# Second half of the reloaded T4: issued from the GpSimd queue instead of the SP queue

## Chip, cores and metric

One Trainium2 chip, one core. The metric is the device time of one execution in microseconds; the median of the runs shown is what counts.

## What is computed

A transformer block on x of 2048 tokens by 1024 features: layernorm, linear attention with 32 heads, residual; then layernorm and a token-mixing MLP (2048 tokens to 3584 hidden units and back), residual. The last part, cut from the reference:

```python
def _B_ref(x, w1, b1, w2, b2):
    h = _layernorm(x, axis=-1)
    u = _gelu(jnp.einsum("bsd,sf->bdf", h, w1) + b1)
    y = jnp.einsum("bdf,fs->bds", u, w2) + b2
    return transpose(y)                      # back to tokens by features
h2 = h + _B_ref(_layernorm(h), B_w1, B_b1, B_w2, B_b2)
```

The change concerns the second product, u with w2, which fills the time from about 390 us to the end.

## The kernel before

The second product is done by a Strassen-like scheme with seven products of half-size blocks (`Product7`, methods p1 to p7). Its moving operands are the two halves of the hidden activation, gE (even rows of 128) and gO (odd rows), and three differences of them, T2, T3 and T4. T2 stays in SBUF (gT2). T3 (product 7) and T4 (product 4) don't both fit: each is computed once, half by half, in `derived`, written to DRAM (tiles called parked), and read back when its product is due. There are two SBUF tiles for them, gs0 and gs1, one per half of the contraction (7 of 14 chunks of 128, 896 KB each); in the profile both are "gs". `reload(m, h)` reads half h of T3 (m = 7) or T4 (m = 4) back into its tile. A reload must wait until PE has read the tile's earlier content.

The outputs come in row blocks of 256 tokens, called p; two of them form a `Quad`. The first quad is done by itself, the other three by `Quad.run2` with u = 1, 2, 3. In run2 two of the seven products of a quad (1 and 5) and two more (2 and 3) are done once more by the same scheme over both row blocks: the inner steps, in order in1, in5, in2, in3. Between the inner matmuls `interleave` fills in the matmuls of products 6, 7 and 4: product 7 (from T3) beside in2, the first half of product 4 (T4, gs0) beside in3, and the second half (T4, gs1) beside in1 of the next quad. For the last quad that second half comes at the very end.

The weights of w2 come in "even" and "odd" rows of 128 interleaved: `even` has two buffers (896 KB each, the tile is called wq), which are reloaded for the next quad by `next2`, as soon as product 7 of this quad has read them, with `load_w2(p, 0, hd)`. In run2 the calls stand in this order, at the end of in2:

```python
            nxt = nxt()          # next2(u + 1): two even weight rows on SP; nothing in the last quad
            load("in2")          # the second half of T4 into gs1
```

Engines are written with prefixes: `hd` is SyncE (SP) with its instructions kept in program order, `nc.gpsimd` is the GpSimd engine (POOL). `Held.__getattr__` (line 230) is the line under which all kept instructions appear. DMAs issued on SP run on the queue that the profile calls q1 hardware_dynamic, those on POOL on q0 software_dynamic.

The outputs are added to the residual, which is already in the output tensor, by accumulating DMAs on POOL (line 484, in `Mixer2.out`): 30 of them, 128 rows of 1 KB each. They go through four output buffers (`ots`, pieces of a wq tile), filled by ScalarE (line 487) or VectorE (line 491). The order of the POOL queue beyond kept instructions is set by the scheduler of the language.

Of the kernel before, what the change touches and what calls it, by code (L numbers as in the profile page):

```python
# [30 lines left out]
def kernel(  # L31
# [12 lines left out]
    nc = tc.nc  # L44
# [116 lines left out]
    def load_w2(p, second, q=nc.sync):  # L161
        q.dma_start(
            (odd[p] if second else even[p % 2]),
            B_w2[:, p * 2 * P:(p + 1) * 2 * P].rearrange("(k two p) s -> p k two s", two=2, p=P)[:, :, second, :],
        )
# [64 lines left out]
            return (lambda *a, **kw: pin(op(*a, **kw))) if self.always or getattr(Held, self.key) else op  # L230

    dve, pe, act = Held(nc.vector), Held(nc.tensor), Held(nc.scalar, key="scalar")
    hv, ht, hs, hd = (Held(e, True) for e in (nc.vector, nc.tensor, nc.scalar, nc.sync))

    class Inner:
        banks = 4
# [1352 lines left out]
    parked = {}  # L1589

    def gs_tile(m, h):
        t = g2pool.tile([P, H2, CW], FP16, tag=f"gs{h}", name=f"gs{h}")
        gs[m, h] = t
        now = [gs.get((m, i)) for i in range(2)]
        gmov[m] = lambda k: now[k // H2][:, k % H2, :]
        return t
# [9 lines left out]

        return [partial(make, h) for h in range(2)]

    def reload(m, h):
        hd.dma_start(gs_tile(m, h)[:], parked[m, h][:])  # L1610

    make_t3 = derived(7, lambda sl: (gT2[:, sl, :], gE[:, sl, 0:CW]))
    make_t4 = derived(4, lambda sl: (gO[:, sl, 0:CW], gT2[:, sl, :]))
# [23 lines left out]
    def loads(u):  # L1637
        def load(at):
            last = 2 * u + 2 >= NSP
            if at == "in1":  # L1640
                if u == 1:
                    reload(7, 0)
                reload(7, 1)
                for p in (2 * u + 2, 2 * u + 3):
                    if 4 <= p < NSP:
                        load_w2(p, 1, hd)
            elif at == "p7":
                reload(4, 0)
            elif at == "in2":
                reload(4, 1)  # L1650
            elif at == "in3":
                if not last:
                    reload(7, 0)
        return load
# [70 lines left out]
```

## Time and profile before

| what | value |
|---|---|
| median of 3 runs | 562.45 us (562.22 to 563.06) |
| the profiled execution's own time | 562.69 us |
| its span, first to last instruction | 560.9 us |
| PE busy | 552.3 us |
| POOL busy | 28.0 us, 30 of its instructions the accumulating stores of 0.93 us mean |
| reloads (gs<-parked) | 12 on SP, 896 KB each, median 5.1 us from issue to landing |
| even weight rows (wq<-in_B_w_dram, 896 KB) | 12 on SP, median 7.2 us |
| accumulating stores (out_dram<-wq, 128 KB) | 30 on POOL, median 6.0 us |

The profile is of one execution, so sums are made against its own time. Instants are microseconds from the start of the span. An engine's row in a timeline is: start, length, engine, line, operation, output<-input, shape, how many, and in square brackets how long the engine idled before it and what released it. For a DMA the length on SP or POOL is that of issuing it, not of moving the data; "to landing" is from its issue to its completion.

### The profile page before, as it was taken

Reading aid. Unit: us, or ns where it says so; the run is one execution under the profiler, and the core shown is the slowest. Engines: PE = TensorE matmul, PEld = TensorE weight load, DVE = VectorE, ACT = ScalarE, POOL = GpSimd, SP = SyncE. Lnnn points to the kernel's source line nnn. Section 1 sums busy time; section 2 is a strip of 40 time slices with the busy share of each in tenths; the row PEclk is TensorE's granted clock in tenths of the full one; section 3 lists DMA queues with packets and bytes.
Section 4 is the critical chain, followed back from the end, with each engine's and each line's share of the span. In section 5 each row is a group of like instructions: output and inputs, shape, how many; then the busy total and the mean of one; then the engine's idle time right before and its main releaser. Section 6 shows DMA issues by size and latency. Waiting matters only on the chain.

```text
span 560.9 us, 8812 instructions
## 1 busy us (share of the span) xinstructions
PE 552.3 (98%) x3323; PEld 316.0 (56%) x3339; DVE 427.6 (76%) x836; ACT 290.8 (52%) x617; POOL 28.0 (5%) x38
## 2 busy tenths in 40 slices
PE   8999999999999999999999999999999999999997
PEld 3444444454444444456666766666445666666665
DVE  6898888544776688889989789888997878648643
ACT  5747677766766877645546465564211412413322
POOL 1000000000000000000000000000002103103112
PEclk9999999999999999999999999999999999999999
DMA  9933332115765851103140340422959749849336
GB/s 306 295 75 76 84 86 39 19 48 194 218 205 134 256 186 76 75 1 106 47 150 24 128 151 1 151 61 72 230 198 284 213 142 295 207 130 282 87 94 132
DMA packets 84203, 77.92 MB, mean 139 GB/s; under 512 B 15666, under 2 KB 76096, under 8 KB 84160
## 3 DMA queue, kind: packets, MB, share of 16 engines
q1 hardware_dynamic: 79104, 72.76, 42.8%
q0 software_dynamic: 4384, 3.95, 4.8%
q10 hardware_dynamic: 672, 0.66, 0.3%
q8 instruction: 26, 0.43, 0.3%
q14 instruction: 17, 0.14, 0.1%
HBM read 61.62 MB, written 12.58 MB: 132 GB/s over the span
## 4 chain that ended last, share of the span: by engine, by line
PE 92%; DMA 4%; DVE 2%; ACT 1%; issue 1%; SPq 0%; DVEq 0%; ACTq 0%
PE psI L230 23%; PE acc_t L230 18%; PE psC L230 14%; PE psB L230 8%; PE psC L940 4%; PE psB L940 4%; PE psA L940 4%; DMA gs<-parked 4%; PE psA L342 2%; PE psB L342 2%; PE acc_t L1226 2%; PE psE L940 2%; PE psC L342 2%; PE acc_t L864 2%; PE psA L230 1%; PE kvps L893 1%
## 5 line engine op out<-in xcount | busy, mean ns | idle before, releaser
L230 PEld LDWEIGHTS <-is 128*128 128x128 f16 x736 | 71.8, 98 | 31.2 <-DVE hi L230 0.4
L230 PEld LDWEIGHTS <-sa 128*128 128x128 f16 x606 | 59.2, 98 | 27.1
L230 PEld LDWEIGHTS <-wq 128*128 128x128 bf16 (+1 forms) x496 | 48.5, 98 | 29.2 <-issue 2.1
L230 PE MATMUL acc_t<-wo_sb,pqT 128*128 128x512 f16 x256 | 55.6, 379 | 0.0
L484 POOL DMA_DIRECT2D out_dram<-wq x30 | 26.1, 931 | 527.4 <-ACT wq L487 497.1
L230 PE MATMUL acc_t<-xnT,wq_sb 128*128 128x512 bf16 x188 | 43.1, 379 | 0.2
L230 PEld LDWEIGHTS <-pqT 128*128 128x128 bf16 x256 | 25.0, 98 | 30.5 <-issue 0.6
L193 DVE TENSOR_SCALAR e_sb<-e_sb 128x512 bf16<-128x512 bf16 x64 | 18.5, 290 | 28.8 <-ACT e_sb L189 28.2
L230 DVE TENSOR_TENSOR t<-psI,t 128x256 f32<-128x256 f32 (+1 forms) x45 | 20.8, 475 | 22.2 <-PE psI L230 21.0
L189 ACT ACTIVATE e_sb<-acc_t 128x512 bf16<-128x512 f32 x40 | 23.9, 597 | 24.5 <-PE acc_t L230 12.0
L230 PE MATMUL psC<-gs,wq 128*128 128x512 f16 x140 | 34.1, 379 | 1.0 <-DMA gs<-parked 1.0
L940 PEld LDWEIGHTS <-xs 128*128 128x128 f16 x208 | 20.0, 98 | 23.3 <-DVE xs L926 1.3
L230 PEld LDWEIGHTS <-wq_sb 128*128 128x128 bf16 x192 | 18.5, 98 | 23.0 <-issue 1.3
L230 PE MATMUL psC<-hT,sa 128*128 128x512 f16 x112 | 31.2, 379 | 0.0
L230 PE MATMUL psI<-hi,is 128*128 128x256 f16 x200 | 30.0, 273 | 0.0
L230 PE MATMUL psB<-hT,sa 128*128 128x512 f16 x112 | 29.7, 379 | 0.0
L230 DVE BATCH_NORM_STATS2 hst<-acc_t 128x6 f32<-128x512 f32 x32 | 21.4, 692 | 9.1 <-ACT h_bf L230 8.9
L940 PE MATMUL psA<-wkv,xnT 128*128 128x512 bf16 x99 | 26.4, 379 | 0.3
L940 PEld LDWEIGHTS <-xnT 128*128 128x128 bf16 x156 | 15.3, 98 | 18.5 <-issue 0.2
L230 DVE TENSOR_TENSOR e<-psI,es 128x256 f32<-128x256 f32 x20 | 8.5, 424 | 21.8 <-PE psI L230 21.8
L230 PE MATMUL psC<-hT,wq 128*128 128x512 f16 x96 | 24.6, 379 | 0.0
L230 ACT CAST h_bf<-acc_t 128x512 bf16<-128x512 f32 x32 | 18.4, 581 | 11.9 <-PE acc_t L230 11.7
(227 smaller groups left out, 1089.9 us busy)
## 6 DMA issues: line engine op xcount, KB each, us to landing
wq<-in_B_w_dram SPq DMA_DIRECT2D x14, 1024.0 KB, 7.8
wq<-in_B_w_dram SPq DMA_DIRECT2D x12, 896.0 KB, 7.2
gs<-parked SPq DMA_DIRECT2D x12, 896.0 KB, 5.1
xr<-in_A_x_dram SPq DMA_DIRECT2D x16, 256.0 KB, 5.2
rdb<-rd_dram SPq DMA_DIRECT2D x32, 128.0 KB, 3.9
out_dram<-h_bf SPq DMA_DIRECT2D x16, 256.0 KB, 2.0
x_sb<-in_A_x_dram SPq DMA_DIRECT2D x15, 256.0 KB, 3.0
out_dram<-wq POOLq DMA_DIRECT2D x30, 128.0 KB, 6.0
```

What stands on the lines that cost most here:

```text
L189: pin(nc.scalar.activation(e_sb[:], src, ACT.Exp))
L193: pin(nc.vector.tensor_scalar(e_sb[:], e_sb[:], 1.0, PHI_EPS, ALU.min, ALU.add))
L230: return (lambda *a, **kw: pin(op(*a, **kw))) if self.always or getattr(Held, self.key) else op
L342: pe.matmul(ps[:, cols], lhsT=lhs[:, k, :], rhs=mv(k)[:, cols], start=(start and k == 0), stop=(k == self.nk - 1), skip_group_check=True,)
L484: nc.gpsimd.dma_start(to, ot[:, a:b], accum_op=ALU.add)
L864: mm = nc.tensor.matmul(pp[:, 0:CW], lhsT=xnT[:, kt, i * P:(i + 1) * P], rhs=wkv[:, kt, c * CW:(c + 1) * CW], start=(kt == 0), stop=(kt == ...
L893: pin(nc.tensor.matmul(kv_ps[b][:, sl, :], lhsT=pks[i % NPK][:, j * P:(j + 1) * P], rhs=vaugs[i % NVA][:, j, :], start=False, stop=(i == N ...
L940: pin(nc.tensor.matmul(ps[:], lhsT=lhs[:, k, :], rhs=rhs[:, k, :], start=(start and k == 0), stop=(k == hk2 - 1), skip_group_check=True,))
L1226: nc.tensor.matmul(qp[:, 0:SW], lhsT=wq_sb[:, kt, j * P:(j + 1) * P], rhs=xnT[:, kt, u * SW:(u + 1) * SW], start=(kt == 0), stop=(kt == ND ...
```

## The change

The second half of T4 is issued with `nc.gpsimd` in place of `nc.sync`. As before, the instruction is kept in program order among the kept ones of its engine; it is the only kind of kept DMA on GpSimd. The tile, its source, its size and what it must wait for stay as they are. It is called three times, for u = 1, 2 and 3. In the last quad no even rows are loaded.

```diff
-    hv, ht, hs, hd = (Held(e, True) for e in (nc.vector, nc.tensor, nc.scalar, nc.sync))
+    hv, ht, hs, hd, hg = (Held(e, True) for e in (nc.vector, nc.tensor, nc.scalar, nc.sync, nc.gpsimd))
...
-    def reload(m, h):
-        hd.dma_start(gs_tile(m, h)[:], parked[m, h][:])
+    def reload(m, h, q=hd):
+        q.dma_start(gs_tile(m, h)[:], parked[m, h][:])
...
             elif at == "p7":
                 reload(4, 0)
             elif at == "in2":
-                reload(4, 1)
+                reload(4, 1, hg)
```

## The prediction

> **What bounds the kernel now.** I read the page's first and fourth parts, then the chain of waits in order of time, then the PE, SP and POOL timelines around its gaps, then the DMA answers in stretches of half a microsecond to two.
>
> ```profile
> span 560.9 us, 8812 instructions
> PE 552.3 (98%) x3323; PEld 316.0 (56%) x3339; DVE 427.6 (76%) x836; ACT 290.8 (52%) x617; POOL 28.0 (5%) x38
> PE 92%; DMA 4%; DVE 2%; ACT 1%; issue 1%; SPq 0%; DVEq 0%; ACTq 0%
> ```
>
> TensorE is busy 98% of the span; only a PE wait removed or added moves the end. The chain names one tile's transfer, and the list of waits gives its true price: "PE psC L230 <- DMA gs<-parked" is 1.9 us, 2 times. The PE timeline has the two places:
>
> ```profile
> 472.53 0.93 PE L230 MATMUL psI<-gE,wq 128*128 128x256 f16 x7
> 474.40 1.02 PE L230 MATMUL psC<-gs,w2o 128*128 128x512 f16 x4 [0.94 <-DMA gs<-parked]
> 515.05 1.02 PE L230 MATMUL psC<-gs,wq 128*128 128x512 f16 x4 [0.97 <-DMA gs<-parked]
> ```
>
> The reader is to see that PE was ready at 473.46 (474.40 less 0.94) and 514.08, and waited for T4's second half, the tile gs1. The 10.34 us that the chain gives this transfer is its whole flight, nearly all beside PE work. The SP timeline shows why it is late:
>
> ```profile
> 458.27 0.34 SPq L230 DMA_DIRECT2D gs<-parked  x1
> 461.31 2.64 SPq L230 DMA_DIRECT2D wq<-in_B_w_dram  x2
> 464.01 8.28 SPq L230 DMA_DIRECT2D gs<-parked  x2
> ```
>
> gs1 is issued at 464.01, right behind two even rows, which land at 466.6 and 471.5 (5.3 and 8.0 us after issue). gs1 lands 10.3 us after issue, though the same 896 KB takes 4.6 to 5.4 us where no row is ahead. The third use has no rows: issued at 544.87 (second line below is POOL's), landed 5.2 us later, needed at 553.99 by the chain. So there is 1.9 us to win in all, 0.34% of the time.
>
> POOL's timeline shows the queue that the transfer moves to:
>
> ```profile
> 463.56 1.75 POOL L484 DMA_DIRECT2D out_dram<-wq  x2 [20.91 <-ACT wq L487]
> 466.47 1.76 POOL L484 DMA_DIRECT2D out_dram<-wq  x2 [1.16 <-ACT wq L487]
> 504.18 1.75 POOL L484 DMA_DIRECT2D out_dram<-wq  x2 [20.68 <-ACT wq L487]
> 507.09 1.75 POOL L484 DMA_DIRECT2D out_dram<-wq  x2 [1.16 <-DMA wq<-in_B_w_dram]
> 544.84 1.75 POOL L484 DMA_DIRECT2D out_dram<-wq  x2 [20.68 <-ACT wq L487]
> 547.75 1.75 POOL L484 DMA_DIRECT2D out_dram<-wq  x2 [1.15 <-ACT psC L403]
> ```
>
> Around each use POOL issues four accumulating stores, in two pairs, at 0.86 us each. The window 549.5 to 552 shows their own pace, with nothing on SP's queue:
>
> ```profile
> q0 software_dynamic: 468, 0.42, 112.5%
> q1 hardware_dynamic: 1, 0.00, 0.0%
> ```
>
> 468 packets in 2.5 us, so about 190 a microsecond; one store is 144 packets (128 rows and 16 more, from 576 for four).
>
> [...] from 471.5 to 473.5 both queues moved 92 packets, rows of 7 KB on q1 against 1 KB on q0. [...] the DMA share of 0.91 to 1.15 from 464 to 478 agrees that there is no idle engine to win. [...] q0's first packets come 4.6 us after the issue at 463.56 (DVE busy from 462.08 to 468.20), but those of the lone store at 554.08, with DVE idle, after about 1.4 us.
>
> **The change part by part.** Three reloads leave SP and join POOL. The two builds have the same instruction order on PE, DVE and ACT. On POOL each reload stands directly behind the four stores above.
>
> *Issue, SP side.* Removed: three issues of about 0.33 us. SP's next work is the reload of T3's first half at about 472.0, which waits for PE. Cover: that wait. Gain 0. The rows gain nothing either, because gs1 stood behind them.
>
> *Issue, POOL side.* POOL is free for it at 466.47 + 1.76 = 468.2 in the first use, 507.09 + 1.75 = 508.8 in the second, 547.75 + 1.75 = 549.5 in the third; on SP it went at 464.0, 504.6 and 544.9. So it is 4.2, 4.2 and 4.6 us later, plus about 0.9 us to issue (nearest row: the stores, also 128 rows). The added wait for PE (the last reader of gs1) is over by 463.4 and costs nothing. Behind the reload on POOL comes a store at 473.75, ahead of which POOL idles 5.5 us: 0.9 us more is covered. Nobody but a later reuse of the four output buffers waits for those stores.
>
> *Flight, first use.* q0 starts at 468.2 and has moved 226 packets by 470.5 (sum of half-microsecond windows), sharing with the rows; the rows run out at about 470.7. From there gs1 no longer stands on q1, so the 576 - 252 = 324 packets left of the four stores run alone: 324 / 190 = 1.7 us, to 472.4. Only then does gs1's turn come in the ring. T3's reload, issued at 472.0, starts about 1 us later (as at 458.27, first packets after 459): gs1 has 0.6 us alone, at 0.4 MB/us (0.42 MB from 475 to 476), so 0.24 MB; then two streams of equal packets share, 0.2 MB/us each, and 0.92 - 0.24 = 0.68 MB takes 3.4 us, to 476.4. With 0.4 us to the semaphore it lands at 476.8 instead of 474.35: **+2.4 us**.
>
> *Second use.* q0 has moved 225 packets by 511.0, where the rows end; 351 left are 1.85 us, to 512.85. T3's reload is issued at about 512.6 and moves from 513.6: 0.75 us alone is 0.3 MB, the other 0.62 MB takes 3.1 us, to 516.7, landing 517.1 instead of 515.0: **+2.1 us**.
>
> *Third use.* Nothing is on q1. The fourth store lands at 554.2 (548.63 + 5.6), with most packets moved by 552.2. gs1 at 0.4 MB/us takes 2.3 us: from 552.2 it ends at 554.5[...]. I take 555.3, against a need at 553.99, where PE waited for nothing before: **+1.3 us**, ahead of only the last 14 matmuls of the chain and the final stores, so no cover is left.
>
> Sum 2.4 + 2.1 + 1.3 = 5.8 us. The profiled execution took 562.69 us (span 560.9 and 1.8 around it), 0.24 above the median of 562.45; from the median the forecast is **568.3 us**. The three waits are bounded from below by -0.94, -0.97 and 0 (PE cannot gain more than it waits), and above by [...] 4.6 us from issue to first packet instead of a free start[...], so some 5 us in all.
>
> **Rivals.**
>
> 1. *The wait is taken away, as the change's words suggest.* [...] For it: an unhindered reload takes 4.6 to 5.4 us. Against it: that is counted from 468.2, not 464.0, and four stores are ahead in the ring. It decides if gs1 lands within 5.2 us of its POOL issue; then the gain is 1.9 us, 560.5, provided the third use lands before 553.99, 4.5 us after issue. Chance 0.05.
> 2. *A wash.* The stores ahead do not hold it and it trades places with the rows' tail: it lands near 474.4 again, and in the third use at 549.5 + 4.6 to 5.4, costing 0.1 to 0.9 us. Time 562.5 to 563.4. [...] Chance 0.10.
> 3. [...] DVE works almost without a gap[...] from 471.66 to 478.66. [...] each of the first two waits grows by 2 to 3 us more: 572 to 575. For it: the 4.6 us delay of the first pair. Against it: DVE idles at 468.20 to 469.14 and 470.36 to 471.32[...]. Chance 0.09.
> 4. That the change does not do what it says is excluded for the issue (the builds show it on POOL), not for "beside the rows": on POOL it starts when the rows are nearly through.
>
> **How the numbers follow.** My forecast has 0.76: 565 to 571, around 568.3. A measurement of this kernel tells about 0.2%, 1.1 us, from no change. Faster is rival 1, 0.05; within 0.2% is most of rival 2, 0.06; slower is 0.76 + 0.04 + 0.09 = 0.89. The range runs from 563.5, the upper end of the wash, to 573[...].
>
> **What would show it.** In the changed profile the reload stands on POOL at about 468.2, behind 466.47; q0 grows by some 2.75 MB; PE's wait for gs is three times, 3.4, 3.1 and 1.3 us instead of twice 0.95; everything between keeps its durations. I am wrong if gs1's flight from POOL is under 5.5 us in the first two uses, if its packets start before the stores have moved, or if the third use has no wait.

## The result, and the profile after

The changed kernel is slower. Its runs took 567.8 and 569.69 us, against a median of 562.45 before: a ratio of 1.011, 95% interval 1.0066 to 1.0154. A third run, of 2079.4 us, is left out, because TensorE ran slow in it from the first matmul to the last (128x512 matmuls of 1.10 us instead of 0.379). Repeated, the changed kernel took 569.88 us, from 566.99 to 571.9 in four runs, against 562.55, ratio 1.0141 (1.0125 to 1.0156). The profile shown is of that repeat, of its execution of 566.99 us, which is the fastest of them.

Its page, first and third parts:

```profile
span 565.2 us, 8832 instructions
PE 552.8 (98%) x3339; PEld 315.9 (56%) x3339; DVE 427.7 (76%) x836; ACT 291.0 (51%) x617; POOL 29.6 (5%) x41
q0 software_dynamic: 4816, 6.70, 6.2%
```

PE's busy time is that of before within 0.5 us, but the span is 4.3 us longer. Queue q0 has grown from 3.95 MB to 6.70, by the three reloads. The PE timeline has three waits for the tile:

```profile
475.08 1.02 PE L230 MATMUL psC<-gs,w2o 128*128 128x512 f16 x4 [1.81 <-DMA gs<-parked]
517.64 1.02 PE L230 MATMUL psC<-gs,wq 128*128 128x512 f16 x4 [2.87 <-DMA gs<-parked]
558.15 3.20 PE L230 MATMUL psC<-gs,w2o 128*128 128x512 f16 x21 [1.57 <-DMA gs<-parked]
```

1.81 + 2.87 + 1.57 = 6.25 us, where before there were 0.94 + 0.97 = 1.91. The difference, 4.3 us, is the whole growth of the span in this execution. The POOL timeline has the place of the reloads:

```profile
463.37 1.75 POOL L484 DMA_DIRECT2D out_dram<-wq  x2 [20.91 <-ACT wq L487]
466.27 1.75 POOL L484 DMA_DIRECT2D out_dram<-wq  x2 [1.15 <-ACT wq L487]
467.45 1.14 POOL L230 DMA_DIRECT2D gs<-parked  x1
```

The reload is issued behind four stores, 3.4 us later than SP did it. The DMA answers for 467.5 to 471.5 and for 471.5 to 473.5 (packets, MB, share of 16 engines) show what its queue does then:

```profile
q0 software_dynamic: 460, 0.43, 67.0%
q1 hardware_dynamic: 879, 0.44, 44.6%
```

```profile
q0 software_dynamic: 211, 0.78, 113.4%
```

Up to 471.5, q0 moves packets of 1 KB only (0.43 MB / 460): stores, beside the last of the rows. The next 211 packets, with q1 empty, have 3.7 KB on average: the last 116 of the four stores' 576, and some 95 of the reload's 128, of 7 KB each. So here the reload's packets follow those of the stores, with little overlap. The reload lands 7.6, 8.7 and 6.7 us after its issue in the three uses.

### The profile page after: what moved, and what is told of

Same layout as the page of the kernel before. It is cut to its first block, busy times and chain, and to the rows that moved or that the text cites. A ratio compares the mean times of both kernels' runs of the same rounds, so it can differ in the third digit from the quotient of the medians.

```text
span 2077.6 us, 8832 instructions
## 1 busy us (share of the span) xinstructions
PE 2073.0 (100%) x3339; PEld 723.1 (35%) x3339; DVE 438.9 (21%) x836; ACT 294.7 (14%) x617; POOL 29.6 (1%) x41
## 4 chain that ended last, share of the span: by engine, by line
PE 100%; DVE 0%; ACT 0%; issue 0%; ACTq 0%
PE psI L230 25%; PE acc_t L230 18%; PE psC L230 16%; PE psB L230 8%; PE psB L940 4%; PE psC L940 4%; PE psA L940 4%; PE acc_t L864 4%; PE acc_t L1226 3%; PE psB L342 2%; PE psA L342 2%; PE psE L940 2%; PE psC L342 2%; PE psA L230 1%; PE kvps L893 1%; PE psE L342 1%
## 5 line engine op out<-in xcount | busy, mean ns | idle before, releaser
L230 PEld LDWEIGHTS <-is 128*128 128x128 f16 x736 | 161.5, 220 | 227.1 <-issue 218.0
L230 PE MATMUL acc_t<-wo_sb,pqT 128*128 128x512 f16 x256 | 210.6, 1103 | 0.0
L230 PEld LDWEIGHTS <-sa 128*128 128x128 f16 x606 | 132.6, 219 | 193.0 <-issue 193.0
L230 PE MATMUL acc_t<-xnT,wq_sb 128*128 128x512 bf16 x192 | 160.5, 1101 | 0.0
L230 PE MATMUL psC<-gs,wq 128*128 128x512 f16 x140 | 122.5, 1112 | 0.0
L230 PE MATMUL psC<-hT,sa 128*128 128x512 f16 x112 | 104.3, 1108 | 0.0
L230 PE MATMUL psB<-hT,sa 128*128 128x512 f16 x112 | 101.7, 1111 | 0.0
L864 PE MATMUL acc_t<-wkv,xnT 128*128 128x512 bf16 x96 | 80.3, 1103 | 0.0
L230 PE MATMUL psI<-gi,is 128*128 128x256 f16 x168 | 75.9, 693 | 0.0
L230 PE MATMUL psB<-gT,sa 128*128 128x512 f16 x84 | 72.4, 1105 | 0.0
```

What stands on the lines that cost most here:

```text
L864: mm = nc.tensor.matmul(pp[:, 0:CW], lhsT=xnT[:, kt, i * P:(i + 1) * P], rhs=wkv[:, kt, c * CW:(c + 1) * CW], start=(kt == 0), stop=(kt == ...
```

## The experiments

**The changed kernel again** (no edit).

> The changed kernel once more, for a profile at the full TensorE rate and for its spread. Theory A (the reload waits its turn in POOL's ring behind four stores, then shares with T3's reload): 566 to 570 us, PE waits for gs three times, about 3.4, 3.1 and 1.3 us; the reload's packets start on q0 only when 576 store packets have moved. Theory B [...]: the waits are as long or longer, but q0 stands still between the last store packet and the first reload packet. Theory C (sharing the 16 engines with the rows is what costs): the rows land later than 5.3 and 8.0 us after issue.

Measured: 569.88 us, waits of 1.81, 2.87 and 1.57 us. Theory A's order holds: stores first, then the reload. B is not needed: between the last store and the first reload packet the queue does not stand still. C does not explain the loss: the rows of the first use do land a little later, 5.7 and 8.2 us after issue against 5.3 and 8.0, but the reload moves nothing before 471.5, where the rows are through, and PE waits for no row. The waits of the profiled run are together 1.5 us shorter than A said, yet the median is 1.6 us above the forecast of 568.3; so the waits are not all. The four runs point to the rest: the mean clock granted to TensorE was 0.999, 0.997, 0.994 and 0.993 in the runs of 566.99, 569.5, 570.25 and 571.9 us. The next experiment shows what lowers it.

**Only the last quad's reload on POOL.**

```diff
-                reload(4, 1, hg)
+                reload(4, 1, hg if last else hd)
```

> Only the last quad's reload goes to POOL, the other two stay on SP behind the rows. Theory A: the first two waits of 0.95 us stay, a third of about 1.3 us (0.6 to 2.2) comes at the end: 563.8 us. Theory C, where the rows are the cost: no rows are loaded in the last quad, so no change, 562.5.

Measured: 566.18 us (563.21 to 567.99), ratio 1.006 (1.0041 to 1.008). C is refuted for this use, since there are no rows to share with. A's wait is there, at 2.23 us just above its bounds, but the loss is 3.6 us and not 1.3. The PE timeline of the profiled execution, and its granted clock (columns: stretch, length, PE busy, PEclk, DMA share, GB/s):

```profile
555.96 4.88 PE L230 MATMUL psC<-gs,w2o 128*128 128x512 f16 x21 [2.23 <-DMA gs<-parked]
```

```profile
554.00:555.00 1.00, 0.00 (x0) 1.00 0.31 129
556.75:557.00 0.25, 0.25 (x3) 1.00 0.96 70
557.00:557.50 0.50, 0.50 (x3) 0.62 1.07 143
560.00:560.40 0.40, 0.40 (x5) 0.50 0.82 276
```

The same 21 matmuls that took 3.20 us in the repeat take 4.88: about 1 us after PE has resumed, its granted clock falls to 0.50, and stays there for 3.4 us. In this execution the wait of 2.23 us costs 1.7 us more after it is over.

**The first two reloads on POOL, the last on SP.**

```diff
-                reload(4, 1, hg)
+                reload(4, 1, hd if last else hg)
```

> The first two reloads go to POOL, the last quad's stays on SP. Theory A: waits of about 3.4 and 3.1 us and none at the end: 567.0 us. Rival (the change's words: beside the rows instead of behind them): 560.5. The losses of this kernel and of the third reload alone should add up to that of the changed kernel.

Measured: 566.83 us (565.17 to 567.67), ratio 1.007 (1.0055 to 1.0084). PE waits 1.71 and 2.73 us, and not at the end. The time is near the 567.0 that A gave, but not by A's waits of 3.4 and 3.1: the two waits are 2.5 us longer than before, and after the second one the granted clock is 0.50 for 3.4 us (518.48 to 521.90), which adds 1.7. The losses of the parts, 3.6 + 4.3, add up to 7.9, near the 7.3 of the whole change. Here too the clock divides the runs: the two with 1.0 took 565.17 and 565.28 us, the four with 0.997 took 566.69 to 567.67.

**The reloads on ScalarE's queue** (q10 in the profile, called hardware_dynamic like SP's q1, but a queue of its own).

```diff
-                reload(4, 1, hg)
+                reload(4, 1, hs)
```

> All three reloads are issued from the ScalarE queue: a queue of its own beside the rows, as in the change, but issued at about 464 and with no stores ahead in its ring. Theory A: gs1 lands before PE needs it (464 plus 6 to 8 us), both old waits go, unless the rows, which now share, land so late that DVE's sums of them make PE wait: 560.5 to 562.5 us. Theory C: the wait moves to the rows in full and nothing is won or it is slower, 562.5 to 565.

Measured: 574.57 us, ratio 1.0212 (1.0199 to 1.0226): the worst of all, outside both expectations. gs1 is in time: PE no longer waits for it. But DVE waits for the rows, and PE for what follows from it. The DVE timeline, the PE timeline, and DMA issues (size, us to landing) near 464:

```profile
476.35 0.62 DVE L230 TENSOR_TENSOR is<-wq 128x896 f16<-128x896 bf16 x1 [3.87 <-DMA wq<-in_B_w_dram]
```

```profile
479.09 1.65 PE L230 MATMUL psI<-gi,is 128*128 128x256 f16 x7 [4.04 <-ACT psI L270]
525.71 1.65 PE L230 MATMUL psI<-gi,is 128*128 128x256 f16 x7 [5.50 <-ACT psI L270]
```

```profile
wq<-in_B_w_dram SPq DMA_DIRECT2D x1, 896.0 KB, 12.0
gs<-parked ACTq DMA_DIRECT2D x1, 896.0 KB, 8.0
```

The second row lands 12.0 us after issue, not 8.0. From 469 to 471.5 the queues moved:

```profile
q10 hardware_dynamic: 114, 0.77, 73.8%
q1 hardware_dynamic: 115, 0.06, 10.0%
```

The packets are equal in number, but one of gs1 is 7 KB and one of a row 0.5 KB. Truly "beside" the rows, the reload takes nearly all the bandwidth (0.77 MB against 0.06), and the row has to move the rest of its packets from 471.5 to 475 beside the four stores. In the kernel before, it landed at 471.58, just before DVE began to read it at 471.66. This is theory C, at several times the price expected, 12.0 us instead of at most 2.5: PE waits 4.04 and 5.50 us, each wait followed by matmuls at a granted clock of 0.50 (1.65 us for seven of them instead of 0.93).

**All three on POOL, ahead of the four stores.** The stores between the last reload of T4's first half and this one are kept back until the reload is issued, and stores stay in program order.

```diff
+    keeping, kept = [False], []
...
-                nc.gpsimd.dma_start(to, ot[:, a:b], accum_op=ALU.add)
+                (kept.append if keeping[0] else lambda f: f())(partial(hg.dma_start, to, ot[:, a:b], accum_op=ALU.add))
...
-                reload(4, 0)
+                reload(4, 0); keeping[0] = True
...
-                reload(4, 1, hg)
+                reload(4, 1, hg); keeping[0] = False; run_all(kept); kept.clear()
```

> All three reloads on POOL as in the change, but ahead of the four stores in its queue. Theory D (a reload truly beside the rows starves the rows, as the ScalarE queue showed): gs1 lands about 8 us after its issue and PE does not wait for it, but the second row lands about 12 us after its own, DVE's sums wait about 4 us and PE after them, twice, and none in the last quad: 573 to 576 us. Rival (the four stores ahead are the whole cost of the change): 560.5 us.

Measured: 572.05 us, ratio 1.0152 (1.0128 to 1.0177), just under the 573 to 576 of theory D. The rival is refuted. The picture is that of ScalarE's queue, a little milder: PE has no wait for gs, DVE waits for the row (3.4 us at the longest) and PE then waits 3.56 and 3.31 us. So in the first two uses, standing behind the stores did not only harm: it also kept the reload off the rows.

**Only the last on POOL, ahead of its stores** (the same edit, `keeping[0] = last` and `hg if last else hd`).

> Only the last quad's reload is on POOL, and ahead of its four stores; the first two stay on SP. No rows are loaded there. If the place behind the stores costs the 1.6 to 2.2 us at the end: 562.5 us, PE waits for gs twice only. If POOL's software queue itself is slow: a third wait of over 1 us stays, 564 to 566.

Measured: 562.45 us against 562.66, ratio 0.9993 (0.998 to 1.0005). POOL issues the reload at 544.83, it lands 5.2 us later, as on SP, and the third wait is gone. In the last quad the place behind the stores is the whole cause; POOL's queue as such costs nothing that these runs can tell.

**First two on POOL, and PE's idle time filled.** The first two reloads are on POOL and the last is on SP, as above. Before each of the two waits PE repeats seven matmuls twice more, which writes the same numbers.

```diff
-            self.mm(1, self.a, True)
-            act.copy(self.b, self.a)
+            for _ in range(1 + Inner.again): self.mm(1, self.a, True)
+            Inner.again = 0; act.copy(self.b, self.a)
...
-                reload(4, 1, hg)
+                reload(4, 1, hd if last else hg)
...
-                    reload(7, 0)
+                    reload(7, 0); Inner.again = 2
```

> The kernel with the first two reloads on POOL; PE repeats the seven matmuls before its wait for gs1 twice more (1.5 us of work that writes the same numbers again), so that it idles about 0.2 and 1.2 us instead of 1.7 and 2.7. Theory E [...]: no stretch with a granted clock of 0.5, 565.2 us with a spread under 0.5. Rival (the transfers themselves land at varying times): no change from 566.8 and its spread of 2.5 us.

Measured: 565.74 us (565.12 to 566.66, seven runs), 1.1 us less than without the 28 extra matmuls. PE idles 0.31 and 0.99 us, the clock is 1.0 in six runs and 0.999 in one, and no run is above 566.66, where four of six were without the filling. The spread is 1.5 us, not under 0.5, and at an unchanged clock it must come from elsewhere; that it comes from the landing times, as the rival says, is likely but was not read run by run. Theory E rests on two profiles, of the third reload alone and of the first two: 2.23 and 2.73 us of idling, each followed by a granted clock of 0.50 for 3.4 us, at 1.7 us each. It holds for the larger part: 1.1 us of the 1.6 that it said.

**A version of the kernel before with the transfer on SP in two parts.**

```diff
-    def reload(m, h):
-        hd.dma_start(gs_tile(m, h)[:], parked[m, h][:])
+    def reload(m, h, cut=H2, t=None): t = gs_tile(m, h); [
+        hd.dma_start(t[:, k, :], parked[m, h][:, k, :]) for k in (slice(0, cut), slice(cut, H2)) if k.start < k.stop]
...
-                reload(4, 1)
+                reload(4, 1, H2 if last else 4)
```

In the first two uses chunks 0 to 3 go first, then chunks 4 to 6; in the last quad the transfer stays whole.

> The kernel before, with the reload of T4's second half on SP as two transfers (4 chunks, then 3), in the first two uses. PE needs only 4 of the 7 chunks at 473.46 and the others 3.3 us later. The first transfer should land some 1 to 1.5 us ahead of where the whole lands now (474.35): both waits of 0.95 us shrink or go, 560.6 to 561.3 us. Rival (the second row's landing is what all waits on): no change, 562.5.

Measured: 561.04 us against 562.66, ratio 0.9969 (0.9959 to 0.998), faster than both kernels. PE waits for gs in neither use. The timeline of the first:

```profile
472.58 0.93 PE L230 MATMUL psI<-gE,wq 128*128 128x256 f16 x7
473.43 1.02 PE L230 MATMUL psC<-gs,w2o 128*128 128x512 f16 x4
```

The first part is issued at 464.06, stays behind the rows, and lands 9.3 us later, at 473.4, just when PE comes to it.

## Why the prediction was right, and where its sum was off

The direction, the place and the number of waits were as forecast, and 569.88 lies in the range; the length of the first wait was not. By its steps:

- *POOL's place.* 468.2 was said, 467.45 is shown; the third at 549.5 against 551.41, on a timeline that was by then 2.6 us late (547.43 against 544.84 for the first stores). Right: the reload stands behind four stores.
- *The order in the queue.* Right, by the packets of 467.5 to 473.5 above.
- *Sharing with T3's reload.* This term failed. It took T3's packets to begin 1 us after issue and to slow gs1 from 473.0. T3's reload was issued at 471.77, but its packets began only at 473.9, when 115 of gs1's 128 packets had begun. The first wait is 1.81 us and not 3.4. In the second use, 2.87 against 3.1, the outcome is close but for other reasons: T3's packets began at 515.3 (issue at 513.27), when 122 of gs1's 128 had begun; all 128 have moved by 516, but the last of the 16 small packets that follow them comes only after 516.5, and gs1 lands at 517.6. Why that one is late is not known.
- *The third use.* 1.3 was said; 1.57 and, alone on POOL, 2.23 us were measured. The first is right within the prediction's bounds; the second is a little over the 0.6 to 2.2 expected of that run. All 21 matmuls of the last block stand behind the wait; the 14 that the prediction named are those in its chain.
- *What was left out.* The prediction took PE's matmuls as unchanged after a wait. The traces show that they can change: with only the third reload on POOL, 2.23 us of idling were followed by 3.41 us at a granted clock of 0.50, and the 21 matmuls took 4.88 us instead of 3.20. In the repeat's profile the clock stays at 1.00 after its three waits. The added waits came to 4.3 us instead of 5.8 in the one execution whose waits were read. The rest of the 7.3 us between the medians goes with the clock: two stretches of 3.41 us at half rate would lower the mean clock over 565 us by 0.006 and cost about 3.4 us (an estimate), and the runs with 0.994 and 0.993 are 3.3 and 4.9 us longer than the one with 0.999. Waits that vary may have a share. That 568.3 comes near 569.9 is thus partly luck, two errors that cancel.
- *Rivals.* The first (the wait goes) had its price right, 1.9 us, but reaching most of it takes another edit, the split on SP (1.6 us). The second, a wash, needed a reload that the stores do not hold; they held it. The third, a reload held up while DVE works, is not supported: in the last quad of the kernel before, POOL issues its first store at 544.84 and q0 moves nothing until about 548.9, 4.1 us later. In the repeat the store is issued at 547.43, with the same instructions on DVE at the same distance (the sum from psB starts 0.36 us ahead of it in both), and q0 has moved 15 packets by 549.0, 1.6 us later. What differs is that gs1 is on q1 in the meantime, in the kernel before alone: 0.82 MB from 544.8 to 548.8, against nothing from 547.0 to 549.0 in the repeat. So the late start goes with the other queue's transfer here, and not with DVE; in what way is not shown.
- *"Beside the rows".* Rightly doubted. But the prediction saw only that this does not happen in the change, not that it would be worse.

## What to carry to other kernels

Before a transfer is moved to another queue, list what stands ahead of it there in the built order, and who needs the bytes that it will now compete with: on ScalarE's queue gs1 and the row moved 114 and 115 packets from 469 to 471.5, of 7 KB and of 0.5 KB, and the row landed 12.0 us after its issue instead of 8.0. When a transfer is late by less than its own length, cutting it so that the first consumer waits for a part (1.6 us won here) disturbed nobody else. A wait of TensorE can cost more than itself: here a stretch of 3.41 us with 2.23 us of idling in it was followed by one at a granted clock of 0.50, which cost 1.7 us more.

## What was not expected of the hardware

- Idle times of 2.23 us (third reload alone) and 2.73 us (first two) on PE were followed by a granted clock of 0.50 for 3.4 us, while others of 2.87 us (the repeat) and 3.56 us (all three ahead of the stores) were not. The length of the wait does not separate the two groups, but its place does. On ScalarE's queue the granted clock changes at 478.64, 482.06, 523.01 and 529.84: 1, 12 and 2 steps of 3.41 us apart. In the kernel before, the record of the granted clock starts at 6.62, and the clock next changes at 559.58, 162 such steps later. The PE busy time and the granted clock in such steps (columns as above), first with only the third reload on POOL, then in the repeat, whose clock does not change near its waits, so that its steps are an estimate, counted on from where its record starts:

```profile
553.71:557.12 3.41, 1.18 (x7) 1.00 0.58 111
557.12:560.53 3.41, 3.41 (x15) 0.50 0.30 65
```

```profile
513.24:516.66 3.42, 1.52 (x14) 1.00 1.05 386
516.66:520.07 3.41, 2.43 (x19) 1.00 0.89 228
```

The wait of 2.23 us lies whole within one step, and the next step has half the clock, though PE has been at work again for 1.2 us when it begins. The wait of 2.87 us falls on an edge of the estimated steps, 1.9 us before it and 1.0 after, and the clock stays at 1.00. That of 3.56 us is split too, 1.97 and 1.59. Steps with 2.23 us of idling or more were found seven times, and each was followed by the half clock: 2.23 (third reload alone), 2.73 (first two), 3.41, 2.80 and 2.70 (ScalarE's queue), 3.09 (all three ahead of the stores), and 2.55 behind the last matmul of the kernel before. The steps of the two split waits, with 1.97 us or less, were followed by a clock of 1.00. Between the two nothing was measured. Where the edges fell against the work differed from trace to trace: the wait of 2.73 us, whole within one step, cost 1.7 us more, and that of 2.87 us, split by the estimate, nothing.
- A reload put on an idle-looking queue started late while another had packets left: on ScalarE's queue gs1 was issued at 464.32, and its first packet moved at about 468.5, while q1 moved 170 to 333 packets in each half microsecond. In the last quad of the kernel before, with gs1 on q1, q0's first packets came about 4 us after POOL's first issue; in the repeat, with nothing on q1, 15 of them had moved 1.6 us after it.
